# An mLSTM cell with a cosine-gated MLP behind it: the head's narrow matmuls widened, its first period written out, its loads reordered, and the division of later cells moved

## The chip, the core and the metric

One core of a Trainium2 chip runs the whole program. The metric is the device time of one execution in microseconds (us), lower is better. The engines are PE (TensorE), ACT (ScalarE), DVE (VectorE), POOL (GpSimd) and SP (SyncE), which here only issues transfers. All inputs and outputs are float32 in device memory; w_in and w_out come as float64 and are turned into float32 on the chip.

## The reference

```python
# q, k, v, o_gate: (B=4, H=8, S=768, D=40); i_gate, f_gate: (4, 8, 768)
for t in range(S):
    m_new = max(f_gate[:, :, t] + m, i_gate[:, :, t])
    f_stab, i_stab = exp(f_gate[:, :, t] + m - m_new), exp(i_gate[:, :, t] - m_new); m = m_new
    C = f_stab * C + i_stab * outer(v_t, k_t)
    n = f_stab * n + i_stab * k_t
    y[:, :, t] = sigmoid(o_gate[:, :, t]) * (C @ q_t) / max(abs(n . q_t), 1)
x = y as (B*S = 3072, H*D = 320)
h = x @ w_in            # w_in (320, 2048)
out = (h * cos(h)) @ w_out   # w_out (2048, 320)
```

## The kernel before

The sequence is cut into NC = 6 chunks of 128 steps. A cell n = 4 c + b is chunk c of batch b with its 8 heads: 24 cells. A cell takes the scores of its 128 steps (`scores`), weighs them with a table of decays E (`decay_exponents`, `decay`, `weigh`), multiplies by the values and adds the part that comes from the state before (`values`), divides and gates (`normalize` or `normalize_turned`), and updates the state (`seam`, `fade`, `state`). Cells 0 to 3 (the first chunk) are the head: they work with tokens on the partitions and turn q, k and the result with TensorE (`turn`, `turn_out`, `seam`). Later cells take q and k turned by DVE in blocks of 32x32 (`turn_blocks`) and leave their heads turned, in `vt`: 128 partitions of dimensions by 3 x 128 columns.

The MLP of chunk c runs while the cells of chunk c + 1 do: `both_parts(c, b)` does two steps f2 of the up-projection `Up(c, f2)` (256 of the 2048 hidden columns each, on all four batches), then for each half near, rest, sin and gate on ACT and DVE, and the down-projection of the step before (`down`, later a form with seven products in place of eight, `sums` and `all_products`). A period is one call of `both_parts`: one cell and two steps.

Four orders decide the times. Everything is under a manual schedule: each engine runs its instructions in the order in which the program writes them. `first_cells` writes the head out by hand, with fillers (`warm(k)`: k matmuls of a zero tile) for PE. The transfers stand in one queue on SP in program order, and a transfer whose buffer is not free stops all behind it. The weights reach float32 in three steps: `take_apart` (ACT), `bound` and `put_together` (DVE), with a last add on POOL; `weights_in(f)` loads one of four parts of w_in (three pieces), `weights_out(p)` one of eight of w_out. Part f serves steps 2f and 2f + 1. Their buffers are few: pool `pb` has two (shared by E3, the decay table of cell 3, and the raw w_in), pool `pc` three (raw w_out and one spare of the gates).

Names that the change touches:

- M0: running maxima of the gates in the first chunk, 32 rows (one for each batch and head). `spread(n, i)` copies rows of it to all partitions by a matmul of a broadcast identity column, for cells 0 and 1, whose E is not loaded.
- `gates_turn`, `gates_keep`: turn the later chunks' gates (columns of 32) by PE and copy them to the table `tab`.
- `pair(t, p)` and PR = 104: two heads side by side, 40 dimensions at offset 0 and 40 at 64. Their tiles are 64 wide for each head, the last 24 zero.
- `turn_gate`: DVE transposes the sigmoid of the o gate to vt's layout, and `normalize_turned` (lines 521 to 537) divides in that layout: maximum on 128x128, reciprocal on 128x128, three shuffles that copy the divisor to the rows, two products.
- `low_dimensions`, `odd_values`, `scale_q`, `clear_low`: small preparations of later cells.
- `sin_next`: a one-element sine that makes ACT load its table early.

Of the kernel before, what the change touches and what calls it, by code (L numbers as in the profile page):

```python
# [11 lines left out]
FP = mybir.dt.float32  # L12
# [4 lines left out]
OP = mybir.AluOpType  # L17
# [12 lines left out]
def kernel(  # L30
# [36 lines left out]
    PR = 64 + D  # L67
# [125 lines left out]
    a0, F0, M0, e0 = p2.tile([128, 4, C], FP, name="first", tag="S")[0:BH].rearrange("r n s -> n r s")  # L193
# [89 lines left out]
    sig, xT, xL, Es, kws, qkT, pss, heads_of, raw_o, Gs, oTs, early = {}, {}, {}, {}, {}, {}, {}, {}, {}, {}, {}, {}  # L283
# [87 lines left out]
    def spread(n, i):  # L371

        for p in range(HP):
            g = n * H + HP * i + p
            nc.tensor.matmul(pm[n, i][:, p], ident[0:BH, g:g + 1].to_broadcast([BH, 128]), M0,
                             start=False, stop=(p == HP - 1))
# [44 lines left out]
    def pair(t, p):  # L421
        return t[:, 2 * p:2 * p + 2].rearrange("p j d -> p (j d)")[:, 0:PR]
# [3 lines left out]
    def turn(n):  # L426

        pool, tag = psum(n)
        pts[n] = []
        for src in (qs(n), ks(n)):  # L430
            pt = pool.tile([128, HP, C], FP, name="pt", tag=tag)
            for p in range(HP):
                nc.tensor.transpose(pt[0:PR, p], pair(src, p), ident)
            pts[n].append(pt)
        qkT[n] = [p1.tile([128, HP, C], FP, name=f"t{i}", tag=f"t{i}") for i in range(2)]
# [20 lines left out]
    def turn_gate(n):  # L456
        c, b = divmod(n, B)
        oTs[n] = p1.tile([128, 3, C], FP, name="oT", tag="oT")
        nc.vector.transpose(out=oTs[n].rearrange("q g (t k) -> q g k t", t=32), in_=sig[c][:, b].rearrange("q (g k) i -> q g k i", g=3))

# [5 lines left out]
    def turn_out(n, on_dve=True):  # L466
        qT, kT = qkT[n]
        nc.scalar.copy(out=qT[0:PR], in_=pts[n][0][0:PR])
        if on_dve:
            nc.vector.tensor_copy(out=kT[0:PR], in_=pts[n][1][0:PR])  # L470
        else:
            nc.scalar.copy(out=kT[0:PR], in_=pts[n][1][0:PR])

    def scores(n):
        pool, tag = psum(n)
        qT, kT = qkT[n]
        ps = [pool.tile([128, HP, C], FP, name="ps", tag=tag) for _ in range(2)]
        for p in range(HP):
            for j in range(2):
                r = slice(64 * j, 64 * j + D)  # L480
                nc.tensor.matmul(ps[j][:, p], kT[r, p], qT[r, p], start=True, stop=True)  # L481
        pss[n] = ps
# [36 lines left out]
    FROM0, FROM1 = 1, 17  # L519

    def normalize_turned(n):
        c, b = divmod(n, B)
        vt = heads_of[n]
        dn = p2.tile([128, C], FP, name="dt", tag="dt")
        nc.vector.tensor_scalar(out=dn, in0=vt[:, 2], scalar1=-TWO_PI, scalar2=TWO_PI, op0=OP.mult, op1=OP.max)
        nc.vector.scalar_tensor_tensor(out=dn, in0=vt[:, 2], scalar=TWO_PI, in1=dn, op0=OP.mult, op1=OP.max)
        yt = p1.tile([128, 3, C], FP, name="yt", tag="yt")
        nc.vector.tensor_tensor(out=yt, in0=vt, in1=oTs[n], op=OP.mult)
        nc.vector.reciprocal(out=dn, in_=dn)
        db = p1.tile([128, 3, C], FP, name="db", tag="db")  # L530
# [5 lines left out]
        nc.vector.tensor_tensor(out=xT[c][:, NK * b:NK * b + NK + 1], in0=yt, in1=db, op=OP.mult)  # L536
        ys[n] = xT[c][:, NK * b + NK]
# [294 lines left out]
    def first_cells():  # L832
# [72 lines left out]
        load_E(B + 1)  # L905
        load_o(1)
# [9 lines left out]
        normalize(2)  # L916
        scores(3)
        pg = gates_turn()
# [24 lines left out]
        load_E(B + 2)  # L943
        ahead.append(weights_in(2))
        decay(B)
        sigmoid(1)
        weigh_k(B)
        odd_values(B)
        scale_q(B)

# [12 lines left out]

    def both_parts(c, b):

        n = (c + 1) * B + b
        cell = n < N
        for i in range(2):
            f2 = 2 * b + i
            up = Up(c, f2)  # L970
            if cell and i == 0:
                scores(n)
                if c == 0 and b == 0:

                    warm(8, psum_o())
# [7 lines left out]
            if i == 0:  # L983
                if cell:
# [3 lines left out]
                    if n == B:  # L988
                        clear_low()
# [3 lines left out]
                if c > 0:  # L993
                    sums(c, f2)
                if b == 0 and c == 1:
                    sigmoid(c + 1)
# [25 lines left out]
            down_slot(c, f2)  # L1022
# [3 lines left out]
            if cell and i == 0:  # L1026
                turn_gate(n)
# [19 lines left out]
            if i == 1:  # L1047
                if c == 0 and ahead:
                    pieces.extend(ahead.pop(0))
                if c == 0 and b == 0:  # L1050
                    ahead.append(weights_in(3))
# [53 lines left out]
```

## Time and profile before

| | us |
|---|---|
| median of 3 runs | 539.55 |
| lowest, highest | 538.50, 540.12 |
| the profiled execution | 540.26 |
| its span, first to last instruction | 538.5 |
| mean granted PE clock | 0.969 |

The page divides the span into 40 slices and gives for each the busy share of the engines and the clock that PE was granted. Groups of instructions are named by line, engine, operation and tile: `pup` is the up-projection, `po`, `acc` and `late` the down-projection, `ps` the scores, `vt` and `ph` the values, `pt` the turned q or k, `pm` the spread maxima, `pg` and `pd` the turned gates, `pw` fillers, `n` and `g` the MLP's elementwise tiles, `bits` and `low` raw weights. The transfers that SP issues are shown as SPq.

### The profile page before, as it was taken

What the parts mean: (1) busy time and instruction counts of PE and PEld (TensorE: products, weight loads), DVE (VectorE), ACT (ScalarE), POOL (GpSimd) and SP (SyncE); (2) the same over time, 40 slices, a digit from 0 to 9 for tenths busy, and PEclk for the clock granted to TensorE, in tenths of its full rate; (3) what the DMA queues carried; (4) which work ended last, traced back from release to release, by engine and by line L of the source; (5) the groups of instructions that cost most, each with busy time, mean ns of one, the idle gap of its engine ahead of it and who ended that gap; (6) DMA issues with size and microseconds to landing.
All of it is one profiled execution on the core that took longest, in us unless ns stands there. A gap on an engine that the chain in (4) does not pass through costs nothing.

```text
span 538.5 us, 10486 instructions
## 1 busy us (share of the span) xinstructions
PE 522.8 (97%) x3844; PEld 354.4 (66%) x3844; DVE 419.5 (78%) x907; ACT 287.1 (53%) x546; POOL 247.8 (46%) x409
## 2 busy tenths in 40 slices
PE   7999979999999999999999999999999999999996
PEld 4885536556666757767767767767657667576755
DVE  5565879897888988898878898878898879663636
ACT  2587949767566537827527826527836522222221
POOL 7435465465665865553553553553432433121211
PEclk9585989999999999999999999999999999999999
DMA  9999969799727539229249229159220000000001
GB/s 137 210 197 231 254 176 179 200 194 215 131 94 174 58 94 193 51 87 194 34 125 175 38 91 195 28 124 167 44 83 7 1 5 6 20 30 1 1 0 49
DMA packets 97762, 57.81 MB, mean 107 GB/s; under 512 B 62048, under 2 KB 89792, under 8 KB 97712
## 3 DMA queue, kind: packets, MB, share of 16 engines
q1 hardware_dynamic: 96240, 55.64, 50.4%
q0 software_dynamic: 1424, 1.49, 1.3%
q8 instruction: 30, 0.49, 0.4%
q14 instruction: 20, 0.16, 0.1%
q10 hardware_dynamic: 48, 0.02, 0.0%
HBM read 51.71 MB, written 4.11 MB: 104 GB/s over the span
## 4 chain that ended last, share of the span: by engine, by line
PE 76%; DMA 10%; DVE 8%; SPq 3%; POOL 2%; ACT 1%; issue 1%; DVEq 0%; POOLq 0%
PE pup L648 27%; PE acc L758 22%; PE pup L642 8%; PE po L680 5%; PE ps L481 3%; DMA bits<-in_moe_w_in_dram 3%; PE late L758 3%; PE vt L516 2%; PE vt L507 2%; DVE t L454 1%; DMA low<-in_moe_w_in_dram 1%; PE pu L599 1%; DMA G<-G_d 1%; DMA bits<-in_moe_w_out_dram 1%; DVE g L668 1%; DMA E<-M_d 1%
## 5 line engine op out<-in xcount | busy, mean ns | idle before, releaser
L648 PE MATMUL pup<-xT,w_in_sb 128*128 128x512 f32 x384 | 178.3, 607 | 4.0 <-POOL w_in_sb L163 2.9
L656 ACT ACTIVATE n<-pup 128x512 int32<-128x512 f32 x96 | 54.1, 595 | 201.7 <-PE pup L642 148.8
L648 PEld LDWEIGHTS pup<-xT,w_in_sb 128*128 128x128 f32 x384 | 70.7, 192 | 91.3 <-issue 84.4
L659 DVE SCALAR_TENSOR_TENSOR n<-pup,n 128x512 f32<-128x512 f32 x96 | 63.1, 687 | 79.6 <-ACT n L656 77.9
L722 POOL TENSOR_TENSOR D<-g 128x128 f32<-128x128 f32 x40 | 19.6, 490 | 138.0 <-DVE g L668 138.0
L664 ACT ACTIVATE n<-n 128x512 f32<-128x512 f32 x96 | 59.3, 630 | 16.0 <-DVE n L659 16.0
L668 DVE SCALAR_TENSOR_TENSOR g<-pup,n 128x512 f32<-128x512 f32 x96 | 62.0, 685 | 2.4 <-ACT n L664 1.7
L758 PE MATMUL acc<-w_out_sb,g 128*128 128x160 f32 x320 | 58.6, 304 | 0.0
L758 PE MATMUL acc<-T,g 128*128 128x160 f32 x320 | 58.0, 301 | 0.1
L642 PE MATMUL pup<-xL,w_in_l 64*128 64x512 f32 x192 | 55.7, 651 | 0.6 <-POOL w_in_l L163 0.6
L605 POOL DMA_DIRECT2D xL<-xT x40 | 22.4, 561 | 72.6 <-DVE xT L536 68.6
L758 PEld LDWEIGHTS acc<-w_out_sb,g 128*128 128x128 f32 x320 | 47.8, 190 | 5.6 <-issue 3.9
L758 PEld LDWEIGHTS acc<-T,g 128*128 128x128 f32 x320 | 48.1, 190 | 3.7 <-issue 3.0
L404 ACT ACTIVATE E<-E,tab 128x128 f32<-128x128 f32 x160 | 49.0, 389 | 0.3
L680 PE MATMUL po<-w_out_sb,g 128*128 128x320 f32 x128 | 36.2, 436 | 0.0
L481 PEld LDWEIGHTS ps<-t,t 40*128 40x128 f32 x384 | 26.4, 198 | 13.5 <-DVE t L454 7.2
L758 PE MATMUL acc<-T,S 128*128 128x160 f32 x160 | 35.0, 301 | 0.0
L680 PEld LDWEIGHTS po<-w_out_sb,g 128*128 128x128 f32 x128 | 24.0, 190 | 11.2 <-issue 1.9
L487 DVE TENSOR_TENSOR E<-ps,E 128x512 f32<-128x512 f32 x48 | 30.7, 681 | 0.5 <-PE ps L481 0.5
L642 PEld LDWEIGHTS pup<-xL,w_in_l 64*128 64x128 f32 x192 | 15.0, 187 | 24.5 <-issue 21.3
L481 PE MATMUL ps<-t,t 40*128 40x128 f32 x384 | 28.7, 289 | 1.1 <-DVE t L454 0.8
L758 PE MATMUL acc<-w_out_sb,S 128*128 128x160 f32 x160 | 28.8, 299 | 0.0
(177 smaller groups left out, 908.6 us busy)
## 6 DMA issues: line engine op xcount, KB each, us to landing
E<-M_d SPq DMA_DIRECT2D x22, 512.0 KB, 3.7
qr<-in_q_dram SPq DMA_DIRECT2D x36, 160.0 KB, 3.5
kr<-in_k_dram SPq DMA_DIRECT2D x36, 160.0 KB, 5.7
G<-G_d SPq DMA_DIRECT2D x20, 256.0 KB, 6.6
bits<-in_moe_w_out_dram SPq DMA_DIRECT2D x8, 640.0 KB, 6.8
bits<-in_moe_w_in_dram SPq DMA_DIRECT2D x16, 256.0 KB, 6.9
out_dram<-o_sb SPq DMA_DIRECT2D x24, 160.0 KB, 1.9
ks<-in_k_dram SPq DMA_DIRECT2D x10, 320.0 KB, 7.9
```

Source lines behind the costliest of these rows:

```text
L404: nc.scalar.activation(out=Es[n][:, h], in_=Es[n][:, h], func=AF.Exp, scale=-1.0, bias=tab[:, c, 0, g:g + 1])
L481: nc.tensor.matmul(ps[j][:, p], kT[r, p], qT[r, p], start=True, stop=True)
L487: nc.vector.tensor_tensor(out=w, in0=pss[n][j], in1=w, op=OP.mult)
L605: nc.gpsimd.dma_start(out=xL[c][64 * e:64 * e + 64, b], in_=ys[n][0:128:2])
L642: nc.tensor.matmul(pu, w_in_l[r, f2], xL[c][r].rearrange("p b t -> p (b t)"), start=ahead, stop=not ahead)
L648: nc.tensor.matmul(pu.rearrange("p (b t) -> p b t", b=B), w_in_sb[:, i, ts(2 * f2 + e, 128)], xT[c][:, i:NK * B:NK], start=(i == 0 and not ...
L656: nc.scalar.activation(out=self.n[e], in_=self.pu[e], func=AF.Copy, bias=0.25)
L659: nc.vector.scalar_tensor_tensor(out=self.n[e].bitcast(FP), in0=self.pu[e], scalar=0.25, in1=self.n[e], op0=OP.add, op1=OP.subtract)
L664: nc.scalar.activation(out=r, in_=r, func=AF.Sin, scale=TWO_PI_DOWN)
L668: nc.vector.scalar_tensor_tensor(out=g, in0=self.pu[e], scalar=TWO_PI, in1=self.n[e].bitcast(FP), op0=OP.mult, op1=OP.mult)
L680: nc.tensor.matmul(po[c][b], gs[c, f][:, ts(b, C)], w_out_sb[:, f], start=(f == 0), stop=(f == NF - 1))
L758: nc.tensor.matmul(a, lhs, rhs, start=start, stop=stop)
```

## The change

The matrices that PE multiplies with in the head get more rows. M0 is now a tile of 128 rows whose rows 32 to 127 are set to zero by DVE, and `spread` uses all 128 rows of the identity. `pair` takes all 128 columns, so `turn` transposes to 128 rows and `turn_out` copies 128. `scores` of cells 0 to 3 uses 64 rows for each head instead of 40 (the rest is zero).

In `first_cells`, `values(3)` moves ahead of `gates_turn`, and `gates_turn` behind `warm(3)`; two fillers are added ahead of `scores(3)` and two behind the turning. The transfers E(B + 1) and o gate of the second chunk move behind w_in(1), and w_in(2) to the end.

The first call of `both_parts` becomes `first_period`, written out: w_in's second part is converted in the middle of the second up step, piece by piece, `sigmoid(1)` and the decay of the next cell come behind that, and the loads of the cell after next move ahead of w_out(3), w_in(3) and w_out(4). `fade(B)` now stands behind `state(B)`. In the next call, step (0, 2) has the down-projection ahead of the scores, and the scores' weighing behind the gate.

`normalize_turned` first transposes the divisor's rows to tokens on the partitions, takes maximum and reciprocal there on 128 x 8, multiplies the sigmoid with it, transposes that product, and multiplies `vt` once. `turn_gate` is gone.

```diff
+    first = p2.tile([128, 4, C], FP, name="first", tag="S")
+    M0_rows = first[:, 2]
+    nc.vector.memset(M0_rows, 0.0)
...
-            nc.tensor.matmul(pm[n, i][:, p], ident[0:BH, g:g + 1].to_broadcast([BH, 128]), M0,
+            nc.tensor.matmul(pm[n, i][:, p], ident[:, g:g + 1].to_broadcast([128, 128]), M0_rows,
...
-                r = slice(64 * j, 64 * j + D)
+                r = slice(64 * j, 64 * j + (64 if n < B else D))
...
     def normalize_turned(n):
...
-        dn = p2.tile([128, C], FP, name="dt", tag="dt")
-        nc.vector.tensor_scalar(out=dn, in0=vt[:, 2], ...)
-        nc.vector.scalar_tensor_tensor(out=dn, in0=vt[:, 2], ...)
-        nc.vector.tensor_tensor(out=yt, in0=vt, in1=oTs[n], op=OP.mult)
+        dt = p2.tile([128, K4, 32], FP, name="dt", tag="dt")
+        nc.vector.transpose(out=dt, in_=vt[:, 2].rearrange("q (t k) -> q k t", t=32))
+        dn = p2.tile([128, K4, 2], FP, name="dn", tag="dn")
+        nc.vector.tensor_scalar(out=dn, in0=dt[:, :, 1:32:16], ...)
+        nc.vector.scalar_tensor_tensor(out=dn, in0=dt[:, :, 1:32:16], ...)
         nc.vector.reciprocal(out=dn, in_=dn)
-        for i, mask in enumerate(([FROM0] * 32, [FROM1] * 32, [FROM0] * 16 + [FROM1] * 16)):
-            nc.vector.stream_shuffle(out=db[:, i], in_=dn, mask=mask)
+        so = p1.tile([128, 3 * K4, 32], FP, name="so", tag="yt")
+        nc.vector.tensor_tensor(out=so[:, 0:2 * K4]..., in0=sig[c][:, b, 0:2 * K4]..., in1=dn..., op=OP.mult)
+        nc.vector.tensor_tensor(out=so[:, 2 * K4:3 * K4]..., in0=sig[c][:, b, 2 * K4:3 * K4]..., in1=dn..., op=OP.mult)
+        nc.vector.transpose(out=oT..., in_=so...)
-        nc.vector.tensor_tensor(out=xT[c][:, NK * b:NK * b + NK + 1], in0=yt, in1=db, op=OP.mult)
+        nc.vector.tensor_tensor(out=xT[c][:, NK * b:NK * b + NK + 1], in0=vt, in1=oT, op=OP.mult)
...
         load_two(B, "Kv")
-        load_E(B + 1)
-        load_o(1)
         outs.append((0, weights_out(0)))
...
+        warm(2)
         scores(3)
-        pg = gates_turn()
         warm(1)
         seam(2)
         weigh(3)
-        to_float32(pieces.pop(0))
-        decay_exponents(B)
+        take_apart(*pieces[0])
+        bound(pieces[0][0])
+        put_together(*pieces.pop(0))
+        values(3)
         pieces.extend(weights_in(1))
-        outs.extend((p, weights_out(p)) for p in range(1, 3))
         seam_out(2)
...
+        warm(3)
+        pg = gates_turn()
+        normalize(3)
         gates_keep(*pg)
-        values(3)
-        normalize(3)
...
-        warm(3)
+        warm(2)
         seam(3)
         seam_out(3)
+        decay_exponents(B)
...
+        load_E(B + 1)
+        load_o(1)
+        outs.append((1, weights_out(1)))
+        load_E(B + 2)
+        outs.append((2, weights_out(2)))
...
-        sigmoid(1)
         weigh_k(B)
         odd_values(B)
         scale_q(B)
+        ahead.append(weights_in(2))
...
+    def first_period():
+        n = B
+        up = Up(0, 0)
+        scores(n)
+        warm(8, psum_o())
+        (near, weigh(n), rest, clear_low, sin and gate, values(n), seam(n))
+        to_float32(outs.pop(0)[1])
+        up = Up(0, 1)
+        take_apart(*pieces[0])
+        take_apart(*pieces[1])
+        bound(pieces[0][0])
+        put_together(*pieces[0])
+        decay_exponents(n + 1)
+        (near and rest)
+        take_apart(*pieces[2])
+        bound(pieces[1][0])
+        put_together(*pieces[1])
+        (sin and gate)
+        bound(pieces[2][0])
+        put_together(*pieces[2])
+        to_float32(outs.pop(0)[1])
+        sigmoid(1)
+        decay(n + 1)
+        state(n)
+        normalize_turned(n)
+        low_out(n)
+        fade(n)
+        turn_blocks(n + 1)
+        scale_q(n + 1)
+        weigh_k(n + 1)
+        sin_next()
+        down(0, 0)
+        pieces.extend(ahead.pop(0))
+        load_two((n + 3) // 2 * 2)
+        load_E(n + 3)
+        outs.append((3, weights_out(3)))
+        ahead.append(weights_in(3))
+        outs.append((4, weights_out(4)))
```

In this listing the lines in brackets stand for the calls they name, in that order.

More of the change, by code (lines that the diff above doesn't have):

```diff
@@ L432, in turn @@
             for p in range(HP):
-                nc.tensor.transpose(pt[0:PR, p], pair(src, p), ident)
+                nc.tensor.transpose(pt[:, p], pair(src, p), ident)
             pts[n].append(pt)
@@ L467, in turn_out @@
         qT, kT = qkT[n]
[L468 to L472, printed above, removed]
+        nc.scalar.copy(out=qT, in_=pts[n][0])
+        (nc.vector.tensor_copy if on_dve else nc.scalar.copy)(out=kT, in_=pts[n][1])
     def scores(n):
@@ L970, in both_parts @@
             up = Up(c, f2)
-            if cell and i == 0:
+            late = (c, f2) == (0, 2)
+            if cell and i == 0 and not late:
                 scores(n)
-                if c == 0 and b == 0:
-                    warm(8, psum_o())
             if cell and i == 1:
@@ L983, in both_parts @@
             if i == 0:
-                if cell:
+                if cell and not late:
                     weigh(n)
@@ L994, in both_parts @@
                     sums(c, f2)
+                if late:
+                    down_slot(c, f2)
+                    scores(n)
+                    weigh(n)
+                    decay_exponents(n + 1)
                 if b == 0 and c == 1:
@@ L1021, in both_parts @@
                 sin_next()
-            down_slot(c, f2)
+            if not late:
+                down_slot(c, f2)
             if f2 == 0 and c > 1:
```

56 lines of the change are left out of this document (36 added, 20 removed).

## The prediction

> **What bounds the kernel now.** I read the page first: busy time of each engine and the granted clock by slices.
>
> ```profile
> span 538.5 us, 10486 instructions
> PE 522.8 (97%) x3844; PEld 354.4 (66%) x3844; DVE 419.5 (78%) x907; ACT 287.1 (53%) x546; POOL 247.8 (46%) x409
> PEclk9585989999999999999999999999999999999999
> ```
>
> PE is busy almost throughout, so it sets the end; but its clock falls to five tenths in slices 2 and 4, with less in their neighbours. Busy time at half clock is not the same as work. Next the stretches, to see where PE has no slack and where its clock was halved (columns: length, busy time of PE, PEld, DVE, ACT, POOL, then clock, DMA share, GB/s).
>
> ```profile
> 200.00:400.00 200.00, 199.69 (x1657) 139.66 (x1656) 169.94 (x387) 113.27 (x214) 96.14 (x173) 1.00 0.53 108
> 14.00:27.10 13.10, 13.10 (x70) 11.46 (x69) 7.45 (x15) 7.66 (x10) 5.52 (x8) 0.50 0.96 219
> 37.90:51.40 13.50, 13.18 (x70) 8.54 (x69) 8.63 (x19) 9.24 (x30) 6.02 (x7) 0.50 1.08 218
> 75.50:78.70 3.20, 3.20 (x8) 1.04 (x8) 1.23 (x2) 0.00 (x0) 3.20 (x3) 0.50 0.19 44
> ```
>
> From 200 to 400 us PE idles 0.31 us at full clock, with DVE 15% free: nothing taken from DVE, ACT or DMA there can bring more than those tenths. All that can move lies ahead of some 100 us: two stretches of 13.1 and 13.5 us at half clock, a third of 3.2, and the waits in the first period. The third view is PE's timeline there (start, duration, instruction, idle time before and its releaser); it gives the pace of the four head cells (L497, the values) and the first period (L648 and L642).
>
> ```profile
> 18.97 3.64 PE L497 MATMUL ph<-vs,E 128*128 128x41 f32 x16
> 28.41 1.98 PE L497 MATMUL ph<-vs,E 128*128 128x41 f32 x16
> 33.35 1.98 PE L497 MATMUL ph<-vs,E 128*128 128x41 f32 x16
> 39.73 3.64 PE L497 MATMUL ph<-vs,E 128*128 128x41 f32 x16
> 43.17 1.48 PE L830 MATMUL pw<-nil 128*128 128x512 bf16 x3
> 46.83 6.02 PE L648 MATMUL pup<-xT,w_in_sb 128*128 128x512 f32 x8
> 74.14 2.56 PE L648 MATMUL pup<-xT,w_in_sb 128*128 128x512 f32 x4 [2.88 <-POOL w_in_sb L163]
> 78.50 1.22 PE L481 MATMUL ps<-t,t 40*128 40x128 f32 x16
> ```
>
> The same 16 matmuls take 1.98 us at full clock and 3.64 at half. From the first up-projection (46.83) to the end of the third (78.50) pass 31.7 us, at the end of which PE waits for a converted weight.
>
> **Part 1, rows filled, cell 3 ahead of the gates' turning.** Where does the clock fall? [...]
>
> ```profile
> 10.60:14.00 3.40, 3.40 (x29) 2.55 (x29) 3.33 (x6) 2.21 (x4) 0.11 (x1) 1.00 0.97 136
> 24.20:27.60 3.40, 3.40 (x16) 2.39 (x14) 2.61 (x5) 1.17 (x2) 0.39 (x1) 0.50 1.06 245
> 34.50:37.90 3.40, 3.30 (x37) 2.82 (x37) 2.84 (x9) 2.82 (x8) 1.98 (x2) 1.00 1.05 234
> 72.00:75.40 3.40, 1.26 (x3) 0.68 (x4) 3.40 (x5) 0.00 (x0) 2.64 (x3) 1.00 0.72 197
> 12.40 1.15 PE L375 MATMUL pm<-first,ident 32*128 32x128 f32 x8
> 24.54 1.09 PE L433 MATMUL pt<-ident,qs 128*104 128x128 f32 x4
> 36.35 0.24 PE L272 MATMUL pg<-ident,qr 32*128 32x32 f32 x1
> ```
>
> The pieces before the falls at 14.0 and 37.9 are busy 3.40 and 3.30 us, yet the clock fell behind both. What fills them are narrow matmuls: the spreading of the maxima with 32 rows, the gates' turning with 32, scores with 40. The piece before the rise at 27.6 is transposes, 128 rows by 104, and two fillers. I read this as: rows that work count. The change gives the spreads 128 rows, the scores 64, the transposes 128, and puts the turning (ten such small ones, about a microsecond) behind cell 3's values and between fillers. [...]
>
> If the clock holds, what is the new start of the up-projection? The first values wait for the weighing on DVE, which the clock does not touch:
>
> ```profile
> 15.66 1.25 DVE L487 TENSOR_TENSOR E<-ps,E 128x512 f32<-128x512 f32 x2
> 1.14 1.15 DVE L117 MEMSET qr<- 128x1312 f32 x1 [0.23 <-issue]
> ```
>
> So values 0 start at about 17.0, not 18.97. Values 1 to 2 took 28.41 to 33.35, 4.94 us a cell at full clock; that is the pace for the rest: 17.0 + 5.9 (the longer first step, with 2 fillers and the third and fourth spreads) + 4.9 + 5.4 (two more fillers) = 33.3 for values 3. From there to the up-projection took 7.1 us at half clock (3.64 + 1.48 + the seam and a wait); at full clock with two more fillers and the turning about 5.5: 38.8. Such a walk leaves out small waits between engines, so I add 2 us: 40.8 instead of 46.83, **6.0 us**. Bounds: 8.0 by the bare walk, and about -1 if the clock falls as before, where four more fillers of 0.49 us each lie on the path, partly where PE waited. The new memset ahead of the first filler is at most an eighth of the row above (128 of 1312 elements): 0.15 us, inside the 2.
>
> **Part 2, the first period written out.** ACT is the engine in question.
>
> ```profile
> 46.30 0.37 ACT L611 COPY xT<-px 128x256 f32<-128x256 f32 x1 [3.20 <-PE px L592]
> 70.68 0.81 ACT L151 ACTIVATE bits<-bits 128x640 int32<-128x640 uint32 x1
> 78.80 1.08 ACT L656 ACTIVATE n<-pup 128x512 int32<-128x512 f32 x2 [7.31 <-PE pup L642]
> 72.76 1.32 POOL L163 TENSOR_TENSOR w_in_sb<-w_in_sb,bits 128x512 int32<-128x512 int32 x1 [3.95 <-DVE w_in_sb L162]
> ```
>
> From 46.30 to 71.5 ACT works through, then idles 7.31 us for the third up-projection, which waits for POOL's put_together at 72.76, which waits for DVE, which waited for ACT: sigmoid, decay and three conversions stood ahead of it. The changed order has the same ACT instructions between the same two points, but takes apart the three pieces first and does sigmoid, decay of the next cell and sin_next last, while PE does the third up-projection. Then about 25.2 us of ACT work remain, plus a wait of 2.1 us for the second up-projection and 0.6 for the rounding on DVE: near of the third comes 27.4 us after the first up-projection starts, not 32.0: **4.5 us**. Bounds: 0 (new waits as long as the old) to 7.3. What is late next: scores of the next cell now stand behind down(0,1), and its weighing behind near, rest, sin and gate of the third. By these steps PE then idles some 3.5 us. The piece 72.0 to 75.4 shows what 1.26 us of work in 3.4 does: half clock, 3.2 us long (1.6 us lost). I take 1.0 off. On POOL the next cell's affine select stands ahead of the second w_in piece, so a late load of E(5) would hold the weights.
>
> **Part 3, loads.**
>
> ```profile
> 47.57 1.75 SPq L171 DMA_DIRECT2D bits<-in_moe_w_in_dram x4
> 62.25 6.08 SPq L176 DMA_DIRECT2D low<-in_moe_w_in_dram x4
> 69.08 8.23 SPq L182 DMA_DIRECT2D bits<-in_moe_w_out_dram x2
> E<-M_d SPq DMA_DIRECT2D x22, 512.0 KB, 3.7
> o<-in_o_gate_dram SPq DMA_DIRECT2D x40, 80.0 KB, 4.1
> 76.00:78.00 2.00, 2.00 (x5) 0.84 (x6) 0.73 (x1) 0.00 (x0) 2.00 (x2) 0.50 0.06 8
> ```
>
> (The last two are from the page's list of issues: size of one in KB.) The DMA share is about 1 in the head (rows above: 0.96 to 1.08), so bytes cannot come earlier in sum; only their order changes. w_in(1) goes ahead of E(5) and the o gate (eight issues): 512 + 8 x 80 KB fewer ahead of it, at 218 GB/s some 5 us, so it is issued from about 42 on instead of 47.6. ACT wants its first part 11 us after the up-projection starts, at 52. It must wait until values 3 free its buffer (at 35 now), and all later loads queue behind that. The third w_in is issued by 68.3 as before, since the bytes ahead are the same; ACT now wants it at about 70.5. That is a margin of 2 us where it was 13, and w_out(1) and the o gate have none: I take **1.0** off. The queue's stop at 69.08 (8.2 us, w_out waiting for a buffer while the DMA fell to 0.06) goes, since cell loads now stand there: that pays for the loads that are wanted earlier in the second period.
>
> **Part 4, division in token layout.**
>
> ```profile
> 60.55 0.88 DVE L459 STREAM_TRANSPOSE oT<-og 128x384 f32<-128x384 f32 x1
> 61.28 0.27 DVE L525 TENSOR_SCALAR dt<-vt 128x128 f32<-128x128 f32 x1
> 63.98 0.56 DVE L536 TENSOR_TENSOR xT<-yt,db 128x384 f32<-128x384 f32 x1
> 98.68 1.10 DVE L454 STREAM_TRANSPOSE t<-qr 128x512 f32<-128x512 f32 x1
> 23.04 0.20 DVE L550 RECIPROCAL dn<-dn 128x8 f32<-128x8 f32 x1
> 23.64 0.56 DVE L556 TENSOR_TENSOR y<-yo,dn 128x256 f32<-128x256 f32 x2
> ```
>
> Now 0.88 + (64.54 - 61.28) = 4.1 us a cell. New: a transpose of 128x128 (0.44, from 1.10 and 0.88 for 512 and 384), three small ones (0.20 each), two multiplications (0.56 to 0.8), transpose 0.88, product 0.56: about 3.1, at most 3.9 with the first transpose at 1.10, since none in this trace reads PSUM. That is 0.2 to 1.0 us of DVE a cell, off the path: PE covers it in every later period. I count 0; at most the 0.3 us idle in 200 us.
>
> **Sum.** 6.0 + 4.5 - 1.0 - 1.0 = 8.5 us. The profiled execution took 540.26 us, 1.76 around its span; 531.8 after. The median of the three runs lies 0.7 lower, 539.55, so I give 531.0.
>
> **Rivals.** *The clock falls as before* (rows do not count, or the new pieces fall under the threshold too): the start moves by -1, the first up-projection stays 2.4 us longer at half clock and eats half of part 2: gain about 1.5, 538.0. [...] Against: the 32-row pieces above. Chance 0.20. [...]
>
> *Transfers set the first period*: w_out(1) or E(5) lands 3 to 4 us after ACT or POOL wants it, and sigmoid, decay and the next near go with it. Gain 5.5, 534.0. For: DMA share 1. Against: the order is that of use. Chance 0.17.
>
> *Slower: the transpose out of PSUM.* No row shows one. DVE has 15% of a 20 us period free, 3 us, after which PE waits for gates: if the new chain takes over 7.1 us a cell instead of 4.1, each further us costs 20 us over 20 cells; at 8 us a cell 18 - 8.5, 549. Against: all its parts have cheap relatives above. Chance 0.05.
>
> The forecast, gain 7 to 11 (528.5 to 532.5), has 0.55; 0.03 stays for the change doing nothing to either part. A measurement of this kernel tells 0.3%, 1.6 us, from no change. Faster: 0.55 + 0.17 + 0.08 of the clock rival = 0.80; same 0.12; slower 0.08, the DVE rival and the clock rival's poor end. The range takes in the clock rival's middle and the bare walk with its discounts: 528 to 538.
>
> **What would show it.** Granted clock 1.00 from 14 to 27 and 38 to 51; first L648 (now L650) at 40 to 42; near of the third up-projection some 27 to 28 us behind it; no idle of 7 us on ACT there; a wait of PE of 3 to 4 us before the second cell's values; the same 200 us between two late periods. Wrong: a half clock before 27, an up-projection later than 45, a wait on a DMA ahead of ACT's conversions, or PE idle over 1 us in the middle.

## The result and the profile after

| | before | after |
|---|---|---|
| median of 4 runs, us | 539.31 | 532.91 |
| lowest, highest | 538.50, 540.12 | 531.87, 534.21 |
| ratio | | 0.9883 [0.9857, 0.9909] |
| the profiled execution, its span | 540.26, 538.5 | 531.87, 530.1 |
| mean granted clock there | 0.969 | 0.988 |

The kernel became 6.4 us faster in the medians, where 8.5 were forecast. The two profiled executions lie 8.4 us apart, because that of the kernel before (540.26) is slower than its four timed runs and that of the changed kernel (531.87) is the fastest of its four. So the traces below differ by 2.0 us more than the medians. The stretches show that the gain came about in another way than forecast.

The page of the changed kernel, its head and the clock row:

```profile
span 530.1 us, 10427 instructions
PE 512.8 (97%) x3848; PEld 346.9 (65%) x3848; DVE 406.9 (77%) x828; ACT 286.6 (54%) x546; POOL 247.9 (47%) x409
PEclk9999879999999999999999999999999999999999
```

The same stretches as before, the changed kernel (length, busy time of PE, PEld, DVE, ACT, POOL, then clock, DMA share, GB/s), with 50 to 60 us and the new fall of the clock, from 75 to 80 us, added:

```profile
14.00:27.10 13.10, 12.44 (x136) 10.96 (x135) 10.85 (x25) 11.45 (x19) 7.82 (x10) 1.00 1.04 236
37.90:51.40 13.50, 13.11 (x132) 6.79 (x127) 10.81 (x16) 10.16 (x24) 8.74 (x9) 1.00 1.11 203
50.00:60.00 10.00, 7.64 (x24) 4.18 (x22) 5.47 (x10) 5.04 (x10) 3.97 (x4) 1.00 0.92 186
75.00:80.00 5.00, 4.68 (x74) 3.96 (x76) 4.90 (x10) 4.97 (x11) 2.25 (x3) 0.50 1.29 164
200.00:400.00 200.00, 199.84 (x1674) 140.43 (x1676) 163.05 (x352) 114.64 (x220) 94.99 (x172) 1.00 0.50 105
```

The head has its full clock, and the first up-projection starts at 38.44 in place of 46.83. But from 50 to 60 us PE is busy for only 7.64 of 10 us, while the DMA share is 0.92. PE's and ACT's timelines say why (start, duration, instruction, idle time before and what ended it):

```profile
38.44 3.67 PE L650 MATMUL pup<-xT,w_in_sb 128*128 128x512 f32 x8 [0.22 <-ACT xT L613]
60.54 5.34 PE L650 MATMUL pup<-xT,w_in_sb 128*128 128x512 f32 x8 [2.89 <-DVE g L670]
75.32 0.65 PE L501 MATMUL vt<-E,vs 128*32 128x128 f32 x8 [2.79 <-DVE E L481]
94.61 1.16 PE L475 MATMUL ps<-t,t 40*128 40x128 f32 x16 [0.21 <-DVE t L456]
53.53 0.66 ACT L148 ACTIVATE w_in_sb<-bits 128x512 f32<-128x512 f32 x1 [4.33 <-DMA bits<-in_moe_w_in_dram]
61.86 0.78 ACT L148 ACTIVATE w_out_sb<-bits 128x640 f32<-128x640 f32 x1 [3.28 <-DMA bits<-in_moe_w_out_dram]
71.30 1.05 ACT L658 ACTIVATE n<-pup 128x512 int32<-128x512 f32 x2
74.40 0.68 ACT L148 ACTIVATE w_in_sb<-bits 128x512 f32<-128x512 f32 x1 [0.54 <-DMA qr<-in_q_dram]
```

ACT stands twice before a conversion whose raw weights have not landed: 4.33 us for w_in(1), 3.28 us for w_out(1). The near of the third up-projection comes at 71.30, 32.9 us behind the start of the first. Before, it took 32.0 us (46.83 to 78.80). So of the 8.4 us that the head gained, 7.5 are left there. PE's wait for the second cell's values (2.79 us) is one of the things that take some of these back: the scores of the third cell (cells are counted here from the first behind the head) stand at 94.61, in place of 100.77 before, 6.2 us earlier. The other 2.2 us of the 8.4 come later, bit by bit.

That rest is found in no busy share, since PE is busy 199.69 of 200 us before and 199.84 after. It shows in the distance of one instruction from itself. PE's timeline, the scores of two cells that follow each other, first of the kernel before and then of the changed one:

```profile
382.50 1.06 PE L481 MATMUL ps<-t,t 40*128 40x128 f32 x16
402.93 1.16 PE L481 MATMUL ps<-t,t 40*128 40x128 f32 x16 [0.63 <-DVE t L454]
```

```profile
374.70 1.06 PE L475 MATMUL ps<-t,t 40*128 40x128 f32 x16
394.57 1.16 PE L475 MATMUL ps<-t,t 40*128 40x128 f32 x16 [0.16 <-DVE t L456]
```

20.43 us against 19.87: in this period PE waits for DVE's transposes of the next q and k. In the period that ends at 301.87 in the kernel before, both take 20.02 us. The long ones come once a chunk, where DVE has the sums of the late down-projection to add to the output ahead of the transposes. The four of them took 20.82, 20.49, 20.48 and 20.43 us before and take 20.18, 20.01, 20.02 and 19.87 now, 2.1 us less in sum. From the third cell's scores (100.77 and 94.61) to those 17 periods later (442.12 and 433.77) lie 341.35 us before and 339.16 after: 2.2 us.

The landmarks of all profiles, read from PE's and ACT's timelines in this way (us; "late" is that stretch of 17 periods; `e1` to `e12` are the experiments below):

| kernel | first up-projection | near of the third | third cell's scores | late | span |
|---|---|---|---|---|---|
| before | 46.83 | 78.80 | 100.77 | 341.35 | 538.5 |
| changed | 38.44 | 71.30 | 94.61 | 339.16 | 530.1 |
| e1 rows back | 37.28 | 73.63 | 96.98 | 339.16 | 532.5 |
| e2 rows alone | 39.14 | 75.29 | 97.28 | 341.06 | 534.7 |
| e3 old division | 38.60 | 72.48 | 95.37 | 341.08 | 532.8 |
| e4 division alone | 42.19 | 76.43 | 99.59 | 339.11 | 535.2 |
| e5 no gate load | 37.30 | 68.79 | 93.94 | 339.45 | 529.7 |
| e6 old first period | 37.29 | 80.00 | 103.16 | 339.19 | 538.7 |
| e7 old loads | 38.60 | 73.89 | 99.82 | 339.19 | 535.3 |
| e8 no fillers | 37.84 | 71.92 | 95.23 | 339.10 | 530.7 |
| e9 compute ahead | 38.20 | 68.56 | 96.14 | 339.53 | 532.0 |
| e10 scores ahead | 38.51 | 69.20 | 96.43 | 339.14 | 531.9 |
| e11 one E less | 38.33 | 70.01 | 94.27 | 339.36 | 530.0 |
| e12 two E less | 41.35 | 69.78 | 95.96 | 339.18 | 531.1 |

The span is the time of the third cell's scores plus 435.1 to 435.9 us with the new division, and plus 437.4 to 437.7 with the old. So two questions are left: what sets the third cell's scores, and what the division is worth.

### The profile page after: what moved, and what is told of

It is laid out like the page before. It is cut to its first block, busy times and chain, and to the rows that moved or that the text cites. A ratio compares the mean times of both kernels' runs of the same rounds, so it can differ in the third digit from the quotient of the medians.

```text
span 530.1 us, 10427 instructions
## 1 busy us (share of the span) xinstructions
PE 512.8 (97%) x3848; PEld 346.9 (65%) x3848; DVE 406.9 (77%) x828; ACT 286.6 (54%) x546; POOL 247.9 (47%) x409
## 4 chain that ended last, share of the span: by engine, by line
PE 81%; DVE 7%; DMA 6%; POOL 1%; issue 1%; SPq 1%; ACT 1%; DVEq 0%; POOLq 0%
PE pup L650 26%; PE acc L760 25%; PE pup L644 8%; PE ps L475 4%; PE po L682 3%; PE late L760 3%; DMA bits<-in_moe_w_in_dram 3%; PE vt L510 2%; PE vt L501 2%; PE pu L601 2%; DMA o<-in_o_gate_dram 1%; PE pw L832 1%; DVE t L456 1%; PE ph L491 1%; DMA bits<-in_moe_w_out_dram 1%
## 5 line engine op out<-in xcount | busy, mean ns | idle before, releaser
L475 PEld LDWEIGHTS ps<-t,t 40*128 40x128 f32 (+1 forms) x384 | 24.2, 187 | 12.6 <-DVE t L456 7.5
```

## The experiments

Each was timed against the kernel before, in the same batch; the times are medians.

**e1: the changed kernel with narrow matrices again.**

```diff
-    M0_rows = first[:, 2]
-    nc.vector.memset(M0_rows, 0.0)
-            nc.tensor.matmul(pm[n, i][:, p], ident[:, g:g + 1].to_broadcast([128, 128]), M0_rows,
+            nc.tensor.matmul(pm[n, i][:, p], ident[0:BH, g:g + 1].to_broadcast([BH, 128]), M0,
-                r = slice(64 * j, 64 * j + (64 if n < B else D))
+                r = slice(64 * j, 64 * j + D)
```

(And `pair` with PR = 104 columns.)

> The changed kernel with its matmuls as narrow as before (spreads of 32 rows, scores of 40, transposes 104 wide); order, loads and division as changed. Theory (rows count for the clock): the clock falls to half in the head again, at about 14 us for 10 to 14 us, the first up-projection starts 5 to 8 us later than 38.4 us (44 to 46), the whole takes 3 to 6 us more than the changed kernel (536 to 539), less than the shift because the loads that ACT waited for in the first period have then landed. Rival (the clock follows how busy PE is, rows do nothing; the new order held it): clock 1.00 from 14 to 27, up-projection at 38 to 39, time as the changed kernel within 1 us.

Measured: 533.57 us, ratio 0.9895 [0.9866, 0.9924]; the changed kernel has 0.9883 [0.9857, 0.9909]. The stretches of its head:

```profile
14.00:27.10 13.10, 12.84 (x149) 11.18 (x147) 10.71 (x24) 11.35 (x19) 7.62 (x10) 1.00 0.99 228
37.90:51.40 13.50, 12.38 (x117) 6.26 (x116) 9.12 (x14) 9.12 (x22) 8.36 (x9) 1.00 1.03 199
```

The clock stays full with 32 and 40 rows, as the rival has it. With the new order the wider rows are not needed for the gain.

**e2: the kernel before with the wide matrices alone.** The same edit, the other way round.

> The kernel before with nothing but the filled rows. Theory (rows count): clock at 1.00 over 14 to 27 us; the gates' turning still stands ahead of cell 3's values, so the clock may fall once at 35 to 38; up-projection at 38.5 to 42 instead of 46.8; the gain in the whole is smaller, 2 to 5 us (534.5 to 537.5), as the old first period is bound by ACT's order and later by loads. Rival (rows do nothing): 539 within 1 us, half clock as before.

Measured: 539.47 us, ratio 0.9991 [0.9971, 1.0011]. The profiled execution (536.44 us, the fastest of its twelve) had a full clock until 50 us and its first up-projection at 39.14, 7.7 us earlier than before. PE and ACT then wait:

```profile
54.67 0.65 PE L507 MATMUL vt<-E,vs 128*32 128x128 f32 x8 [7.23 <-issue]
49.27 1.28 ACT L320 ACT_TABLE_LOAD   x1 [5.32 <-DMA o<-in_o_gate_dram]
```

ACT's sigmoid of the second chunk waits for its o gate, with the MLP's work queued behind it, and PE gives back 7.23 us. In this profile the faster head alone brings the third cell's scores 3.5 us forward (97.28 against 100.77); over the twelve runs no gain shows, where 2 to 5 us were expected.

**e3: the changed kernel with the old division; e4: the kernel before with the new one.** `normalize_turned` and `turn_gate` exchanged, nothing else.

> The changed kernel with the old division (sigmoid turned first, maximum and reciprocal on 128x128, three shuffles). Theory (the new division frees about 1 us of DVE a cell, and the later periods, which looked bound by PE alone, get 0.1 to 0.4 us shorter each): 1.5 to 2.5 us more than the changed kernel, a period between two scores of 19.2 us against 18.95 in the second chunk. Rival (division is off the path, as predicted; the 2.2 us between 95 and 400 us come from something else): same as the changed kernel within 0.7 us.

> The kernel before with nothing but the new division. Theory: 1.5 to 2.5 us less than before (537 to 538), all of it gained evenly between 80 and 400 us, head unchanged (up-projection at 46.8). Rival: within 0.7 us of before.

Measured: e3 534.64 us, 0.9914 [0.9891, 0.9936]; e4 538.95 us, 0.9996 [0.9979, 1.0014]. In the totals these say little, but the late column does: 341.08 and 339.11 us. Three profiles with the old division have 341.06 to 341.35, eleven with the new one 339.10 to 339.53. In every profile, then, the new division is worth some 2 us of that stretch. In e4's total it doesn't show, against its expectation (537 to 538 us), though its trace has it. That trace is of the fastest run of twelve (537.0 to 539.96 us), so what takes the 2 us in the others stays open. The other half of that expectation, an unchanged head, failed too: e4's first up-projection comes at 42.19 and not at 46.8, though its head is that of the kernel before (more on this at the end).

**e5: the changed kernel without the load of the second chunk's o gate** (640 KB; its sigmoid is taken of its own buffer, so the second chunk is gated with other numbers).

```diff
+        if c == 1:
+            return
         raw_o[c] = p1.tile([128, B, 2 * C // 32, D], FP, name="o", tag="o")
```

> The changed kernel without the eight transfers of the second chunk's o gate (640 KB); the sigmoid of that chunk reads the buffer that it writes, so the second chunk is gated with other numbers; every instruction on the engines stays. Theory (the first period waits for bytes: ACT stood 4.3 us for w_in(1) and 3.3 us for w_out(1)): w_out(1) lands some 3 us earlier, ACT's wait for it falls from 3.3 us to under 1, near of the third up-projection goes from 71.3 to 68 to 69 us, the whole 1.5 to 3 us less (530 to 531.5). Rival (ACT's own work or the chain of PE and DVE sets it, the wait was slack): same as the changed kernel within 0.7 us.

Measured: 531.00 us, 0.9860 [0.9840, 0.9881]. The median lies 1.9 below that of the changed kernel, but the two intervals overlap, so the total is not shown to be shorter. ACT's timeline:

```profile
59.34 0.79 ACT L148 ACTIVATE w_out_sb<-bits 128x640 f32<-128x640 f32 x1 [1.01 <-DMA bits<-in_moe_w_out_dram]
73.73 0.72 ACT L148 ACTIVATE w_in_sb<-bits 128x512 f32<-128x512 f32 x1 [1.46 <-DMA bits<-in_moe_w_in_dram]
```

The wait for w_out(1) shrinks from 3.28 to 1.01 us and near of the third comes 2.5 us earlier, but then ACT waits 1.46 us for w_in(2), where the changed kernel waits 0.54 us. The third cell's scores gain only 0.7 us.

**e6: the changed kernel with the old order of the first period (and of step (0, 2) in the call behind it), e7: with the old order of loads.**

```diff
     def both_parts(c, b):
-        if (c, b) == (0, 0):
-            first_period()
-            return
...
+                    if n == B:
+                        sigmoid(1)
```

```diff
         load_two(B, "Kv")
+        load_E(B + 1)
+        load_o(1)
         outs.append((0, weights_out(0)))
...
         pieces.extend(weights_in(1))
+        outs.extend((p, weights_out(p)) for p in range(1, 3))
...
-        load_two((n + 3) // 2 * 2)
-        load_E(n + 3)
         outs.append((3, weights_out(3)))
-        ahead.append(weights_in(3))
         outs.append((4, weights_out(4)))
+        ahead.append(weights_in(3))
+        load_two((n + 3) // 2 * 2)
+        load_E(n + 3)
```

> The changed kernel with the old order of the first period (the general call; the sigmoid of the second chunk behind the next cell's decay, since its load is late now), loads, head, rows and division as changed. Theory (the loads' order is what helps, ACT's order only fits it): 1 to 4 us more than the changed kernel, near of the third up-projection at 72 to 76 us, now held by ACT's conversions and not by loads. Rival (ACT's order is nothing, all waits are for loads): within 0.7 us.

> The changed kernel with the old order of loads (E(5) and the o gate ahead of w_out(0) and w_in(1); w_out(1) and w_out(2) next; cell loads behind w_out(3), w_out(4) and w_in(3)). Theory (loads set the first period): w_in(1) lands 5 us later, ACT waits for it until about 58 us, the whole takes 3 to 6 us more (536 to 539), near all of the change's gain gone. Rival (bytes have slack): within 1 us of the changed kernel.

Measured: e6 539.47 us, 1.0012 [0.9999, 1.0026]; e7 537.35 us, 0.9966 [0.9943, 0.9990]. First e6 (ACT, POOL, PE), then e7 (ACT):

```profile
59.07 2.44 ACT L406 ACTIVATE E<-E,tab 128x128 f32<-128x128 f32 x8 [8.55 <-POOL E L392]
57.94 1.09 POOL L392 TENSOR_SCALAR_AFFINE_SELECT E<-E 128x1024 f32<-128x1024 f32 x1 [11.36 <-DMA E<-M_d]
62.87 7.22 PE L682 MATMUL po<-w_out_sb,g 128*128 128x320 f32 x16 [9.15 <-POOL w_out_sb L162]
```

```profile
53.61 0.78 ACT L148 ACTIVATE w_out_sb<-bits 128x640 f32<-128x640 f32 x1 [5.63 <-DMA bits<-in_moe_w_out_dram]
59.52 0.66 ACT L148 ACTIVATE w_in_sb<-bits 128x512 f32<-128x512 f32 x1 [4.45 <-DMA bits<-in_moe_w_in_dram]
```

With the old period the decay of the next cell stands ahead of the conversions, and its E now loads late: POOL waits 11.36 us for it, ACT 8.55, PE 9.15. With the old loads E(5) and the o gate come early, and ACT waits 5.63 and 4.45 us for weights. e6 costs more than its theory allowed for (6.6 us above the changed kernel's median, near of the third at 80.00), e7 what its theory said. The early gain is there only when both orders fit each other: scores at 94.61 with both, 99.82 with the new period alone, 103.16 with the new loads alone, all with the new head and the new division. The new orders with the old head were not tried.

**e8: the changed kernel with one filler at the start and none in the rest of the head.**

> The changed kernel with one filler matmul in place of the 12 at the start and none of the others in the head (the 8 in the first period stay). Theory (loads set the first period, PE's pace in the head is slack): the clock is at half for much of the head, the up-projection starts 2 to 6 us later than 38.4, but near of the third up-projection stays within 1.5 us of 71.3 and the whole within 1.5 us of the changed kernel. Rival (PE's clock in the head sets the time, as the prediction had it): the whole later by as much as the up-projection, 3 to 6 us.

Measured: 533.14 us, 0.9895 [0.9876, 0.9915], as the changed kernel. The half clock and the later up-projection that were expected did not come: the clock is 1.00 from 14 to 27.1 us and 0.98 from there to 37.9 without the fillers, and the first up-projection starts at 37.84, 0.6 us earlier, which is worth nothing. So the run does not tell what a slow head would cost.

**e9: ACT's and DVE's own work ahead of the two waits** (near of the second up-projection ahead of w_in(1), the next cell's decay ahead of w_out(1), its transposes ahead of the division), **e10: e9, and the next cell's scores and weighing ahead of the gate and the down-projection.**

```diff
         up = Up(0, 1)
-        take_apart(*pieces[0])
-        take_apart(*pieces[1])
-        bound(pieces[0][0])
-        put_together(*pieces[0])
         decay_exponents(n + 1)
         (near and rest)
+        take_apart(*pieces[0])
+        bound(pieces[0][0])
+        put_together(*pieces[0])
...
+        decay(n + 1)
         to_float32(outs.pop(0)[1])
         sigmoid(1)
-        decay(n + 1)
         state(n)
+        turn_blocks(n + 1)
         normalize_turned(n)
```

> The changed kernel with another order in its first period: near of the second up-projection ahead of the conversions of w_in(1) on ACT, the next cell's decay ahead of w_out(1)'s conversion, the next cell's turn_blocks ahead of the division on DVE; loads as changed. Theory (work that was ready stood in ACT's queue behind waits for loads): near of the second up-projection at 53.2 instead of 55.8, third up-projection starts at 57.5 to 59 instead of 60.5, its near at 68 to 69.5 instead of 71.3, the whole 1.5 to 3 us less than the changed kernel (530 to 531.5). Rival (the loads of the second period, w_in(2) at 74, hold everything anyway): within 0.7 us of the changed kernel.

> As the one before it, and in step (0, 2) the scores of the next cell and their weighing stand ahead of the sine, the gate and the down-projection, as in the kernel before. Theory: PE's wait of 2.8 us before the second cell's values goes, and with it the half clock from 75 to 80 us; another 0.5 to 2 us less. Rival: scores now wait for turn_blocks and the down-projection behind them comes late; nothing gained, or up to 1 us lost.

Measured: e9 534.15 us, 0.9922 [0.9895, 0.9949]; e10 533.94 us, 0.9913 [0.9882, 0.9945]. In e9 near of the third comes 2.7 us earlier (68.56), but ACT's timeline of e9 goes on:

```profile
62.53 0.78 ACT L148 ACTIVATE w_out_sb<-bits 128x640 f32<-128x640 f32 x1 [1.04 <-DMA bits<-in_moe_w_out_dram]
75.71 0.70 ACT L148 ACTIVATE w_in_sb<-bits 128x512 f32<-128x512 f32 x1 [2.58 <-DMA bits<-in_moe_w_in_dram]
```

w_in(2) is not there: the wait has only moved on, and the third cell's scores come at 96.14, no earlier than in the changed kernel. In e10 PE's wait of 2.8 us is gone, but it waits 2.31 us for DVE within the second cell's scores instead, and the third cell's come at 96.43. Neither gains, as the rivals have it.

**e11: the changed kernel with the table E of the third head cell made on PE by spread maxima, as for the first two, in place of its load of 512 KB, and without the head's later fillers; e12: the fourth cell's E too.**

```diff
-    SPREAD = (0, 1)
+    SPREAD = (0, 1, 2)
...
-        warm(2)
+        spread_up(2)
...
-        decay_exponents(2)
+        for i in range(2):
+            decay_exponents_half(2, i)
```

> The changed kernel, with the decay table E of cell 2 built on PE by spread matmuls as those of cells 0 and 1 are, in place of its 512 KB load, and with the head's later fillers left out, since PE gets the spreads instead. Theory (the bytes wanted by the end of the second period set the first two periods): 512 KB at some 220 GB/s are 2.3 us, so w_in(1), w_out(1) and w_in(2) land about 2 us earlier; ACT's two waits (4.33 and 3.28 us in the changed kernel) shrink by some 2 us in sum, the near of the third up-projection comes at 69 to 70 us and the total is 1.5 to 2.5 us below the changed kernel (530.4 to 531.4). Rival (the head is not slack any more once PE has 16 spreads more, or PE's other waits take it): up-projection later than 40 us and a total within 0.7 us of the changed kernel.

> As the run before, with the E of cell 3 built on PE as well: 1024 KB less to load ahead of the first up-projection. Theory (bytes): another 2 us of the two waits goes, until ACT's own work or PE's 2.8 us more sets the pace; total 2 to 4 us below the changed kernel (529 to 531). Rival (PE or DVE of the head sets it): no better than the run before, with the first up-projection at 41 us or later and ACT waiting there for PE instead of for a DMA.

Measured: e11 531.75 us, 0.9873 [0.9850, 0.9896]; e12 532.31 us, 0.9874 [0.9850, 0.9897]. The medians lie 1.2 and 0.6 us below the changed kernel; the intervals overlap nearly whole, so neither is shown to be faster. In e11 the loads do come earlier: ACT waits 0.36 us for w_in(1), and near of the third comes 1.3 us earlier. Where these 1.3 us end, in the timelines of ACT, DVE, POOL and PE of e11:

```profile
50.67 0.69 ACT L148 ACTIVATE w_in_sb<-bits 128x512 f32<-128x512 f32 x1 [0.36 <-DMA bits<-in_moe_w_in_dram]
60.54 0.79 ACT L148 ACTIVATE w_out_sb<-bits 128x640 f32<-128x640 f32 x1 [3.75 <-DMA bits<-in_moe_w_out_dram]
89.36 0.79 ACT L148 ACTIVATE w_out_sb<-bits 128x640 f32<-128x640 f32 x1 [0.84 <-DMA bits<-in_moe_w_out_dram]
90.18 0.50 DVE L154 TENSOR_SCALAR w_out_sb<-w_out_sb 128x640 f32<-128x640 f32 x1 [1.34 <-ACT w_out_sb L148]
91.67 1.20 POOL L162 TENSOR_TENSOR w_in_l<-w_in_l,low 128x256 int32<-128x256 int32 x1 [4.81 <-DVE w_in_l L161]
92.92 1.13 PE L644 MATMUL pup<-xL,w_in_l 64*128 64x512 f32 x4 [1.62 <-POOL w_in_l L162]
```

The next w_out is late for ACT at 89.36. On DVE the last step of w_in's low rows stands behind w_out's first two, so PE's low rows wait 1.62 us where they waited 0.68 in the changed kernel. The scores gain 0.3 us. In e12 the first up-projection starts only at 41.35, as the rival has it, and the scores come at 95.96. The total is the same although the head ends 2.9 us later.

e12 also shows what holds this stretch when the loads do not. ACT converts w_in(1) and w_out(1) there without a wait, and the third cell's scores come no earlier. First ACT and PE of e12, then 60 to 95 us (columns as above) of e12 and of the changed kernel:

```profile
53.84 0.67 ACT L148 ACTIVATE w_in_sb<-bits 128x512 f32<-128x512 f32 x1
60.33 0.79 ACT L148 ACTIVATE w_out_sb<-bits 128x640 f32<-128x640 f32 x1
73.37 1.23 ACT L666 ACTIVATE n<-n 128x512 f32<-128x512 f32 x2 [2.54 <-DVE n L661]
95.96 1.16 PE L475 MATMUL ps<-t,t 40*128 40x128 f32 x16 [0.23 <-DVE t L456]
```

```profile
60.00:95.00 35.00, 29.77 (x163) 16.62 (x164) 32.77 (x64) 26.96 (x51) 18.62 (x24) 0.95 1.03 205
60.00:95.00 35.00, 30.77 (x162) 16.96 (x164) 31.11 (x61) 27.30 (x52) 19.39 (x25) 0.85 1.07 234
```

DVE is the busiest engine in these 35 us, 32.77 in e12 and 31.11 in the changed kernel, ACT waits for it, and the scores wait for its transposes. So earlier weights meet a DVE that has little time left. No run takes work off DVE there, so this is read from the traces and not shown by an experiment.

## Why the prediction came out, point by point

The forecast was 531.0 us, in 528 to 538; the median is 532.91. The number held, though the gain is 6.4 us and not 8.5, below the 7 to 11 that had the chance of 0.55. Its account did not hold: by the signs that the prediction set for itself, a wait on a DMA ahead of ACT's conversions means that it is wrong, and that wait came (4.33 and 3.28 us). The total lies in the range in part by luck: a loss that was left out (the loads, in part 2) and a gain that was counted as nothing (the division) went in opposite directions.

**Part 1** (6.0 us). The clock held, and the first up-projection came at 38.44, so the bare walk's 38.8 was right and the 2 us added for small waits was not. Of the 8.4 us between the profiles, only 3.8 are left against e4, which has the old head and starts at 42.19. Two steps failed. The reading that rows count is not borne out as the reason for the full clock: e1 keeps it with narrow rows, and e4, whose head is that of before, had clock 1.00 from 14 to 27 us where before's profile had 0.50. The mean granted clocks of e2's twelve runs are 0.979 to 0.990, those of before's 23 runs in the same batch 0.975 to 0.984, so wide rows may help the clock in the old order; which part of the new order keeps the clock in e1, I did not try (with wide rows it is not the fillers, by e8). In the profiles of before and e4 the clock of one and the same head falls at different places (0.50 from 14.00 to 27.10 us in one, 0.66 from 27.10 to 37.90 in the other), and no run shows over what length, or from where, the clock is decided: the rows of 3.40 us in the prediction show no more than what PE did ahead of each change of the clock. DVE's weighing did not follow that clock: in the kernel before, an instruction of its weighing (L487) took 0.65 to 0.69 us in the head's first stretch of half clock and 0.68 to 0.69 in the full clock behind it. The second step that failed is to add the 6.0 us of the start whole to the sum: e2 has 7.7 us at the start, and over its runs no gain.

**Part 2** (4.5 us, to 27.4 us from the first up-projection to near of the third). Measured 32.9, so it brought -0.9 at this point. ACT's order does what it should, and the idle time of 7.31 us there is gone. The step that failed is the sum of ACT's work "plus a wait of 2.1 us for the second up-projection and 0.6 for the rounding": the two waits for loads, 7.6 us, were left out of it. Taken away, they leave 25.3. But the term can't be judged alone: without this order the earlier head is lost entirely (e6, 1.0012 of the time before).

**Part 3** (-1.0 us). The issue of w_in(1) came at 42.55, as predicted ("from about 42"), and ACT wanted it 10.8 us behind the first up-projection, as predicted (11). What failed is the margin: it was counted from the issue, and no landing was worked out. ACT stood waiting for it, and from issue to use it took 11 us, at a DMA share of 1.11 in 37.9 to 51.4. Since the start moved by 8.4 us and not by 6.0, it was also wanted at 49.2 and not at 52. And w_out(1) was issued only at 57.15, behind the o gate's eight transfers, when ACT was 1.4 us from wanting it (SP's queue of the changed kernel):

```profile
42.55 1.75 SPq L170 DMA_DIRECT2D bits<-in_moe_w_in_dram  x4
49.54 7.55 SPq L310 DMA_DIRECT2D o<-in_o_gate_dram  x8
57.15 0.42 SPq L181 DMA_DIRECT2D bits<-in_moe_w_out_dram  x1
```

So the rival *transfers set the first period* came true, in its own figure: w_out(1) was 3.28 us late, within its 3 to 4. Its price was 534.0, and with the division's 2 us it would have been 532.0, close to what was measured. e7 shows that the order of the loads counts. Moving computation ahead of a late load (e9, e10) brings the wait back at the next load; taking bytes away (e5) brings less than 1 us at the third cell's scores and meets the next load as well. Where order and bytes are those of the changed kernel, the third cell's scores follow w_out(1): from its conversion to them lie 32.75 us in the changed kernel (61.86 to 94.61), and 32.77 in e1, whose load was 2.35 us later (64.21 to 96.98). Where it comes earlier (e5, e11, e12) the distance grows to 34.60, 33.73 and 35.63 us, and most or all of what the load gains is lost again; in e12 no load is waited for there, and DVE has hardly any time free. So the loads set the first period; that DVE sets what comes behind them is read from the traces, as said above.

**The discount of 1.0 for PE's idle time.** Forecast 3.5 us before the second cell's values and then half a clock; measured 2.79 us, and 0.50 from 75 to 80. e10 has no such wait and gains nothing; there PE waits 2.31 us within the scores and ACT 2.57 us for w_in(2).

**Part 4** (0). The chain itself came out as worked out: 3.1 us a cell in the groups of 100 to 500 us (below, the first and the largest of eight), against 4.4 for the old groups. The transpose out of PSUM takes 0.32 us, so the rival that fears it fell.

```profile
L521 DVE STREAM_TRANSPOSE dt<-vt 128x128 f32<-128x128 f32 x18 | 5.7, 317 | 3.6 <-PE vt L510 3.3
L534 DVE STREAM_TRANSPOSE oT<-so 128x384 f32<-128x384 f32 x18 | 15.7, 870 | 0.6
```

The failed step is "PE covers it in every later period". It doesn't in one of four: there DVE's transposes end as PE needs them, and the period was about half a microsecond longer. "At most the 0.3 us idle in 200 us" took the idle time of the trace for all that PE can lose. Only the period that ends at 402.93 shows its wait as idle time (0.63 us). In the other two long ones from 200 us on the view shows PE busy throughout, so the half microsecond that they lost must lie inside rows that are shown as busy.

**The clock rival** (538) did not occur, and no run shows the threshold that it speaks of. In sum: forecast 6.0 + 4.5 - 1.0 - 1.0 + 0 = 8.5; measured in the profiles 6.2 up to the third cell's scores, for head, period and loads together, and 2.2 behind them, where the division is. The medians have 6.4 in place of these 8.4, and no run shows in which of the parts the 2 us between them lie.

## What to carry to other kernels

Where the DMA is full (here a share of 1.11 from 37.9 to 51.4 us), an earlier start upstream is worth only what the landing of the next loads allows: for each load write down its landing (issue plus the measured time to land), not its issue, beside the moment when it is wanted. And look which engine is full right behind the load (here, read from the traces, DVE with 32.77 of 35 us in e12); it can take what an earlier landing gains. Change the order of the consumer and the order of its loads together; here one alone brought 1.0 us and the other -2.4 at the third cell's scores, and both 6.2, against the profile of the kernel before. And read a period's length from one instruction's start to its next: busy shares of 99.8% hid half a microsecond in every fourth period.

## What the runs showed of the hardware

Two small operations on DVE took five and nine times their usual time beside POOL's integer adds. These 128 x 8 operations of the division take 0.17 us in the median of 20; in the second cell they took this (DVE, then POOL, of the changed kernel):

```profile
79.09 0.92 DVE L523 TENSOR_SCALAR dn<-dt 128x8 f32<-128x8 f32 x1
80.05 1.49 DVE L524 SCALAR_TENSOR_TENSOR dn<-dt,dn 128x8 f32<-128x8 f32 x1
```

```profile
78.24 1.75 POOL L162 TENSOR_TENSOR w_in_sb<-w_in_sb,bits 128x512 int32<-128x512 int32 x1 [2.75 <-DVE w_in_sb L161]
79.95 1.56 POOL L162 TENSOR_TENSOR w_out_sb<-w_out_sb,bits 128x640 int32<-128x640 int32 x1
```

Both end within 0.03 us of the POOL instruction beside them (80.01 and 79.99, 81.54 and 81.51). In the whole trace five of the 40 (two a cell) overlap such an add (from 65.90, 79.09, 80.05, 102.36 and 103.08 us, 0.60 to 1.50 us long), and each ends 0.02 to 0.03 us behind one. What holds them there no run shows. The old division has two operations of 128x128 on `vt`, which is in PSUM, in these places; in the kernel before they took 0.26 to 0.29 us in all 20 cells, and in the first (61.28 and 61.58) both ran inside one of POOL's integer adds (60.78 to 62.35). The two rows above cost 2 us in the second cell's division, and such long ones are rare later (the means of the two from 100 to 500 us are 0.21 and 0.24 us).

The clock of the head was not a fixed property of the program: with the same head, the profile of before has 0.50 from 14.00 to 27.10 us and 0.97 from there to 37.90, and e4 has 1.00 and 0.66 there, with the first up-projection at 42.19 in place of 46.83 (its stretches, columns as above):

```profile
14.00:27.10 13.10, 12.82 (x148) 11.16 (x146) 10.73 (x24) 11.35 (x19) 7.62 (x10) 1.00 0.96 222
27.10:37.90 10.80, 10.64 (x94) 9.41 (x89) 6.00 (x13) 9.21 (x24) 3.38 (x3) 0.66 1.06 200
```
